# The first chunk of an attention-and-GLU kernel, taken through its first products in two halves

## The chip, the cores and the metric

One NeuronCore of one Trainium2 chip runs the whole kernel. The metric is device time in microseconds (us) of one execution; three executions of the kernel before took 2569.12, 2570.12 and 2572.28 us, median 2570.12. Engines are called as in the profile: PE is TensorE, with PEld its weight loads, DVE VectorE, ACT ScalarE, POOL GpSimd, SP SyncE, whose queue issues nearly all DMAs.

## The reference, cut to what matters

```python
# x: 1 x 2048 x 576, wqkv: 576 x 1728, wo: 576 x 576, H = 32 heads of 18
# w_gate, w_up: 576 x 4608, w_down: 4608 x 576
xn = layernorm(x)                       # over the 576 features, eps 1e-5
q, k, v = split(xn @ wqkv)              # per head
s = softmax(q @ k.T * 18 ** -0.5) @ v @ wo
g = silu(((xn @ w_gate) * (xn @ w_up)) @ w_down)
out = x + s * g
```

## The kernel before

All products run in a 32-bit matmul format, with each factor split into a high part (the copy that the engine's rounding leaves) and a low part (what is missing). A product of two split factors is three products, high by high, high by low and low by high; over the 576 features, in 4 slices of 128 and one of 64, `PAIRS` lists 14 of them.

The program has three stages. The prologue normalises x, turns it so that features lie on the partitions, and computes q, k and v of all rows. It goes by chunks of 512 rows (`NCH` = 4), each four tiles of 128 rows, and by nine blocks of 128 q and k columns. The main stage, from about 200 us on, runs scores, softmax, values and the GLU's products on PE in an order that a planner inside the kernel works out from assumed durations. The last stage multiplies by wo and adds. The change touches the first chunk of the prologue alone, where each engine takes its instructions in the order in which the program writes them.

Before, chunk 0 goes through these steps. `load_x(c)` fetches four tiles of x (L269), `w_fetch(i)` the raw weights of two blocks, `w_last(i, at, b)` one 64-row rest of a block's weights. `norm(0)` takes the tiles one after another: `norm_stats` (L278 to L280) has DVE's statistics and ACT's square root, `norm_apply` (L288 to L292) DVE's reciprocal and scale, ACT's normalised tile `xn` and POOL's copy of its last 64 columns. `w_now(0)` splits the weights of blocks 0 and 1: for these two DVE makes the high part (L428), POOL the low part (L431). `to_columns(0)` turns the tiles: 20 transposes of 128 x 128 (L325), tile by tile, into five PSUM banks; then for each of the five feature slices ACT copies the bank into the high part of `xcx` (L337, L341) and DVE subtracts for the low part (L338, L342). Then `w_now(1)` splits blocks 2 and 3 (ACT L430, POOL L431), `norm(1)` normalises chunk 1, and in the loop over chunks `qk_block(b, 0)` for b = 0, 1, 2 runs 14 products of 512 columns each (L348), ACT's copy of the bank (L351), DVE's subtraction (L352) into `hl`, and the write of `hl` to DRAM (`sqk`, L358). `to_columns(1)` turns chunk 1 (L334), and blocks 3 to 5 of chunk 0 follow. `v_split` and `v_block` (L393, L394, L402) are the value weights and products.

The low parts of one block's weights and the rest of block 1 are read by its last five products:

```python
PAIRS = ([(i, i) for i in range(4)] + [(i, 4 + i) for i in range(4)] + [(8, 8)]
         + [(4 + i, i) for i in range(4)] + [(9, 8)])
```

Of the kernel before, what the change touches and what calls it, by code (L numbers as in the profile page):

```python
# [20 lines left out]
FT = mybir.dt.float32  # L21
FR = mybir.dt.float32r
I32 = mybir.dt.int32
AF = mybir.ActivationFunctionType
OP = mybir.AluOpType
# [15 lines left out]
def kernel(  # L41
# [10 lines left out]
    nc = tc.nc  # L52
    _, S, D = x.shape
# [8 lines left out]
    scale = float(DH) ** -0.5  # L62
# [9 lines left out]
    xcp = ctx.enter_context(tc.tile_pool(name="xcp", bufs=2))  # L72
# [12 lines left out]
    def bank(tag, bufs, k=None):  # L85
        if tag == "g":
            if k is None:
                k = turns[0] = (turns[0] + 1) % 4
            return psum.tile([128, 512], FT, name="pg", tag=f"g{k}", bufs=1)
        return psum.tile([128, 512], FT, name="p" + tag, tag=tag, bufs=bufs)  # L90
# [4 lines left out]
    ident = consts.tile([128, 128], FT, name="ident")  # L95
# [158 lines left out]
    xcs = [None] * NCH  # L254
    vstack, pro, early = ExitStack(), ExitStack(), ExitStack()
    ep = early.enter_context(tc.tile_pool(name="early", bufs=1, side="right"))
# [4 lines left out]
    pp = pro.enter_context(tc.tile_pool(name="pro", bufs=1))  # L261
    blocks = [0, 512, 128, 640, 256, 768, 384, 896, 1024]
    wq = {}
    xin, xns = {}, {}

    def load_x(c):
        xin[c] = ep.tile([128, 4, D], FT, name="xin", bufs=2)
        for t in range(4):
            nc.sync.dma_start(xin[c][:, t, :], x2[c * 512 + t * 128:c * 512 + t * 128 + 128, :])  # L269

    stat = {}

    def norm_stats(c, t):
        st = ep.tile([128, 2, 6], FT, name="st", bufs=4)
        mv = ep.tile([128, 2], FT, name="mv", bufs=4)
        rs = ep.tile([128, 3], FT, name="rs", bufs=4)
        for g in range(2):
            nc.vector.bn_stats(st[:, g, :], xin[c][:, t, g * HALF:(g + 1) * HALF])  # L278
        nc.vector.bn_aggr(mv, st)
        nc.scalar.activation(rs[:, 0:1], mv[:, 1:2], AF.Sqrt, bias=eps)  # L280
        stat[c, t] = mv, rs
# [18 lines left out]
    def norm(c, ts=range(4)):  # L300
        lag = 1 if c in FIRST else len(ts)
        for t in ts:
            norm_stats(c, t)
            if t - lag in ts:
                norm_apply(c, t - lag)
        for t in ts[-lag:]:
            norm_apply(c, t)

    nqk = [0]

    def to_columns(c):

        xn = xns.pop(c)
        if c < 2:
            xc = pp.tile([128, 9, 512], FR, name="xcx", bufs=2)
        else:
            xc = xcp.tile([128, 9, 512], FR, name="xc")
        xcs[c] = xc
        ps = {}
        if c == 0:  # L320
            for k in range(5):
                ps[k] = bank("g", 3) if k < 4 else bank("a", 2)
            for t in range(4):
                for k in range(5):
                    nc.tensor.transpose(ps[k][:, t * 128:(t + 1) * 128], xn[:, t, k * 128:(k + 1) * 128], ident)  # L325
        for k in range(5):
            if c:
                if k in (3, 4):
                    ps[k] = bank("a" if nqk[0] % 2 else "b", 2)
                    nqk[0] += 1  # L330
                else:
                    ps[k] = bank("g", 3)
                for t in range(4):
                    nc.tensor.transpose(ps[k][:, t * 128:(t + 1) * 128], xn[:, t, k * 128:(k + 1) * 128], ident)  # L334
            p = ps[k]
            if k < 4:
                nc.scalar.activation(xc[:, k, :], p, AF.Copy)  # L337
                nc.vector.tensor_tensor(xc[:, 4 + k, :], p, xc[:, k, :].bitcast(FT),  # L338
                                        op=OP.subtract)
            else:  # L340
                nc.scalar.activation(xc[:, 8, :], p, AF.Copy)  # L341
                nc.vector.tensor_tensor(xc[64:128, 8, :], p[64:128, :],  # L342
                                        xc[64:128, 8, :].bitcast(FT), op=OP.subtract)
    def qk_block(b, c):
        p = bank("a" if nqk[0] % 2 else "b", 2)
        nqk[0] += 1
        for n, (a, e) in enumerate(PAIRS):
            nc.tensor.matmul(p, wq[b, a], xcs[c][:, e, :], start=n == 0,  # L348
                             stop=n == len(PAIRS) - 1)
        hl = pp.tile([128, 2, 512], FR, name="hl", bufs=3)  # L350
        nc.scalar.activation(hl[:, 0, :], p, AF.Copy)  # L351
        nc.vector.tensor_tensor(hl[:, 1, :], p, hl[:, 0, :].bitcast(FT), op=OP.subtract)  # L352
        g0 = blocks[b]
        for kind in range(2):
            lo, hi = max(g0, kind * D), min(g0 + 128, (kind + 1) * D)
            if lo < hi:
                dst = sqk[kind, :, lo - kind * D:hi - kind * D, c * 512:(c + 1) * 512]
                nc.sync.dma_start(dst.rearrange("h r s -> r h s"), hl[lo - g0:hi - g0].bitcast(FT))  # L358


    def x_part(b, part):
        return divmod(2 * b + part, 9)
# [61 lines left out]
    def w_piece(i, at, n, b, k0, src):  # L424

        w, low = w_tile(i)
        if i == 0 and b < 2:
            nc.vector.tensor_copy(w[:, at:at + n, :], src)  # L428
        else:
            nc.scalar.activation(w[:, at:at + n, :], src, AF.Copy)  # L430
        nc.gpsimd.tensor_tensor(w[:, low + at:low + at + n, :], src, w[:, at:at + n, :].bitcast(FT), op=OP.subtract)  # L431
        for k in range(k0, k0 + n):
            wq[b, k if k < 4 else 8] = w[:, at + k - k0, :]
            wq[b, 4 + k if k < 4 else 9] = w[:, low + at + k - k0, :]

    def w_now(i):
        at = 0
        for b, n in WHOLE[i]:
            w_piece(i, at, n, b, 0, raws[i][:, at:at + n, :])
            at += n  # L440
# [8 lines left out]
    def w_last(i, at, b):  # L449

        raw = ep.tile([128, 1, 128], FT, name="wl", bufs=2)
        w_load(raw, b, 4, 5)
        return lambda: w_piece(i, at, 1, b, 4, raw)

    def x_store(c, ks):
        for k in ks:
# [3 lines left out]
            else:  # L460
                for part in range(2):
                    nc.sync.dma_start(sx[c, 8, :, part, :], src[64 * part:64 * part + 64])

    def x_first(b, part):

        i, k = x_part(b, part)
        j, r0 = (4 * part + b // 2, 64 * (b % 2)) if b < 8 else (8, 64 * part)
        for r in (0, 64):
            nc.sync.dma_start(xg[i][r:r + 64, k, :].bitcast(FT), xcs[0][r0:r0 + 64, j, :].bitcast(FT))

    raws = {}
    load_x(0)
    w_fetch(0)
    last1 = w_last(2, 9, 1)
    load_x(1)
    w_fetch(1)
    last3 = w_last(2, 10, 3)
    norm(0)
    w_now(0)
    last1()  # L480
    to_columns(0)
    w_now(1)
    norm(1)
    last3()
# [3 lines left out]
    for c in range(NCH):  # L488
        if c + 2 < NCH:
            load_x(c + 2)  # L490
        for b in range(3):
            qk_block(b, c)
        if c + 1 < NCH:
            to_columns(c + 1)
        if c == 0:
            w_now(2)
            last5()
        for b in range(3, 6):
            qk_block(b, c)
            if b < 5 and c + 2 < NCH:  # L500
                norm(c + 2, (0, 1) if b == 3 else (2, 3))
            if c in (1, 2):
                x_store(c, range(3 * (b - 3), 3 * (b - 2)))
            if (c, b) in ((0, 3), (1, 3)):
                v_split(c)
            if (c, b) == (0, 5):
                v_fetch(1)
            if c == NCH - 1 and b == 3:
                w_now(3)
        if c == 1:  # L510
            w_fetch(3)
            for t in range(4):
                v_block(t)
            w_fetch(4)
            last7 = w_last(4, 5, 7)
        if c == 2:
            w_now(4)
            last7()
# [37 lines left out]
    n = 8  # L556
# [21 lines left out]
    with ExitStack() as mid:  # L578
# [240 lines left out]
        def high(k, c):  # L819
            if k == 0:  # L820
                hi[c] = fin["ep"].tile([128, 5, 512], FR, name="hi", bufs=2)
            nc.scalar.activation(hi[c][:, k, :], lo[k][:, 512 * c:512 * c + 512].bitcast(FT), AF.Copy)

        def low(k, c):
            part = lo[k][:, 512 * c:512 * c + 512]
            if k < 4:
                nc.vector.tensor_tensor(part, part.bitcast(FT), hi[c][:, k, :].bitcast(FT), op=OP.subtract)
            else:
                nc.vector.tensor_tensor(hi[c][64:128, 4, :], part[64:128].bitcast(FT), hi[c][64:128, 4, :].bitcast(FT),
                                        op=OP.subtract)  # L830
# [67 lines left out]
        turn = {"a": 0, "b": 0}  # L898
# [300 lines left out]
    ep = fin["ep"]  # L1199
# [63 lines left out]
    ps = {t: banks_of(t) for t in range(4)}  # L1263
# [6 lines left out]
    for t in range(NT):  # L1270
# [5 lines left out]
        for _ in range((2, 0, 0, 0, 2, 2, 1, 0, 2, 2, 1, 0, 0, 0, 0, 0)[t]):  # L1276
            if split:
                k, c = split.pop(0)
# [35 lines left out]
```

## Time and profile before

| | us |
|---|---|
| median of three executions | 2570.12 |
| the profiled execution | 2571.43 |
| its span in the trace | 2569.4 |
| PE busy in the span | 2547.8 (99%) |
| identity ready (DVE, L259) | 1.38 |
| first instruction of PE | 6.79 |
| last product of chunk 0's blocks 0 to 2, start of chunk 1's transposes | 23.23 |

Times below are us from the start of the span. A row of the timeline gives the start, the time it covers, the engine, the line, the operation with its output and inputs, and how many it merges; in brackets stands the idle time before it and what ended it. A line with "L" is a line of the kernel before. PE's matmuls are pipelined: the distance between the starts is what one costs in a stream, and the single duration is longer.

### The profile page before, as it was taken

The page shows a single profiled execution, that of the slowest core. Times are in us where ns is not written, and L with a number is a line of the kernel's source. Part 1 is how long each engine was busy: PE and PEld are TensorE (multiplying, and loading weights), DVE is VectorE, ACT ScalarE, POOL GpSimd, SP SyncE. Part 2 cuts the span into 40 slices and gives each one's busy share as a digit, 9 for nine tenths or more (in the row PEclk, how much of TensorE's full clock was granted, in tenths as well). Part 3 has the DMA queues.
Part 4 walks back from the last instruction along what each step waited for, and adds up shares of the span by engine and source line. Part 5 has one row for each costly group of instructions (what it writes and reads, how often), then busy time and mean ns, then how long its engine had stood idle before and what let it go on. Part 6 is the DMA issues. An engine that isn't in the chain of part 4 may idle for free.

```text
span 2569.4 us, 59203 instructions
## 1 busy us (share of the span) xinstructions
PE 2547.8 (99%) x24360; PEld 2111.1 (82%) x24360; DVE 1933.2 (75%) x3377; ACT 1467.1 (57%) x2688; POOL 594.8 (23%) x663
## 2 busy tenths in 40 slices
PE   8999999999999999999999999999999999999999
PEld 7899888878878888877888888777888877888878
DVE  6208778777778898777778888777888887778437
ACT  5222666666756665555665665555665655556651
POOL 3214434434421111111111111111111111111125
PEclk9999999999999999999999999999999999999999
DMA  7799988888886666665686656665686666654567
GB/s 243 235 284 278 263 226 225 232 225 220 221 206 186 176 182 177 175 179 155 179 197 173 179 175 184 176 170 154 179 204 166 180 184 176 175 174 146 159 189 248
DMA packets 195898, 504.58 MB, mean 196 GB/s; under 512 B 58112, under 2 KB 116352, under 8 KB 156588
## 3 DMA queue, kind: packets, MB, share of 16 engines
q1 hardware_dynamic: 185676, 489.05, 68.6%
q0 software_dynamic: 9952, 11.74, 1.7%
q8 instruction: 192, 3.15, 0.6%
q14 instruction: 78, 0.64, 0.1%
HBM read 312.21 MB, written 107.61 MB: 163 GB/s over the span
## 4 chain that ended last, share of the span: by engine, by line
PE 95%; DMA 3%; DVE 1%; SPq 0%; ACT 0%; issue 0%; POOL 0%; ACTq 0%; DVEq 0%
PE pg L678 34%; PE pg L639 18%; PE pg L720 16%; PE pa L596 12%; PE pb L628 8%; PE pg L402 2%; PE pa L348 2%; PE pb L348 2%; PE pg L1244 1%; DMA hx<-hs 1%; PE pb L1244 1%; PE pa L1244 1%; DMA sqk<-hl 0%; DMA ring<-sqk 0%; DMA xc<-sx 0%; DMA o<-sot 0%
## 5 line engine op out<-in xcount | busy, mean ns | idle before, releaser
L598 DVE TENSOR_REDUCE mx<-pa 128x1 f32<-128x512 f32 x2048 | 1367.1, 686 | 223.6 <-PE pa L596 104.8
L630 ACT ACTIVATE pt<-pb 128x512 f32<-128x512 f32 x2048 | 1161.9, 598 | 534.8 <-PE pb L628 465.5
L678 PE MATMUL pg<-xc,wgu 64*128 64x512 f32 x7776 | 1366.1, 388 | 0.7 <-DMA xc<-sx 0.5
L678 PEld LDWEIGHTS pg<-xc,wgu 64*128 64x128 f32 x7776 | 1051.7, 184 | 41.6 <-DMA xc<-sx 1.2
L628 PE MATMUL pb<-pair,ring 64*128 64x512 f32 x1997 | 777.4, 395 | 1.5 <-DMA ring<-sqk 1.5
L596 PE MATMUL pa<-pair,ring 64*128 64x512 f32 x2006 | 776.9, 393 | 1.8 <-DVE mx L598 1.8
L720 PE MATMUL pg<-wd,hs 64*128 64x288 f32 x3408 | 523.4, 292 | 0.0
L720 PE MATMUL pg<-wd,hx 64*128 64x288 f32 x3408 | 515.2, 292 | 2.4 <-DMA hx<-hs 2.4
L694 POOL TENSOR_TENSOR hs<-us,hs 128x512 fp32r<-128x512 f32 x144 | 186.2, 1293 | 1320.3 <-ACT hs L693 1285.6
L720 PEld LDWEIGHTS pg<-wd,hs 64*128 64x128 f32 x3408 | 459.8, 185 | 4.0 <-DVE acc L748 0.2
L720 PEld LDWEIGHTS pg<-wd,hx 64*128 64x128 f32 x3408 | 453.4, 185 | 6.5 <-DMA hx<-hs 3.0
L639 PE MATMUL pg<-pt,vt 128*32 128x512 f32 x4096 | 454.8, 594 | 0.7 <-DVE acc L748 0.6
L596 PEld LDWEIGHTS pa<-pair,ring 64*128 64x128 f32 x2006 | 364.3, 184 | 69.8 <-issue 52.8
L628 PEld LDWEIGHTS pb<-pair,ring 64*128 64x128 f32 x1997 | 362.5, 184 | 8.7 <-issue 1.9
L639 PEld LDWEIGHTS pg<-pt,vt 128*32 128x32 f32 x4096 | 125.5, 110 | 284.0 <-issue 278.9
L748 DVE TENSOR_TENSOR acc<-acc,pg 128x288 f32<-128x288 f32 x544 | 233.0, 443 | 22.4 <-PE pg L720 21.4
L645 DVE TENSOR_TENSOR oc<-oc,pg 128x512 f32<-128x512 f32 x69 | 47.1, 683 | 220.4 <-PE pg L639 213.7
L693 ACT ACTIVATE hs<-us 128x512 fp32r<-128x512 f32 x144 | 91.0, 632 | 151.0 <-DVE us L690 149.7
L194 POOL TENSOR_TENSOR wgu<-wraw,wgu 128x384 fp32r<-128x384 f32 x108 | 108.6, 1017 | 97.1 <-ACT wgu L193 84.6
L643 ACT ACTIVATE oc<-pg 128x512 f32<-128x512 f32 x32 | 19.2, 598 | 185.0 <-PE pg L639 179.0
L690 DVE TENSOR_TENSOR us<-pg,us 128x512 f32<-128x512 f32 x144 | 98.2, 682 | 26.9 <-PE pg L678 15.7
L618 POOL DMA_DIRECT2D pair<-mt x128 | 77.8, 613 | 166.4 <-DVE mt L613 162.3
(141 smaller groups left out, 1359.0 us busy)
## 6 DMA issues: line engine op xcount, KB each, us to landing
wgu<-swg SPq DMA_DIRECT2D x102, 1152.0 KB
hx<-hs SPq DMA_DIRECT2D x142, 512.0 KB
wd<-swd SPq DMA_DIRECT2D x50, 1152.0 KB
swg<-wgu SPq DMA_DIRECT2D x36, 1152.0 KB
pair<-sqk SPq DMA_DIRECT2D x192, 144.0 KB
ring<-sqk SPq DMA_DIRECT2D x384, 72.0 KB
swd<-wd SPq DMA_DIRECT2D x18, 1152.0 KB
sqk<-hl SPq DMA_DIRECT2D x32, 512.0 KB
```

The costliest lines, as they stand in the source:

```text
L194: nc.gpsimd.tensor_tensor(w[:, 9 + b:12 + b, :], raw[:, b:b + 3, :], w[:, b:b + 3, :].bitcast(FT), op=OP.subtract)
L348: nc.tensor.matmul(p, wq[b, a], xcs[c][:, e, :], start=n == 0, stop=n == len(PAIRS) - 1)
L596: nc.tensor.matmul(p, q[rows, t * 128:(t + 1) * 128], k[rows, c * 512:(c + 1) * 512], start=True, stop=True)
L598: nc.vector.tensor_reduce(mx[h][:, t, c:c + 1], p, axis=AX.X, op=OP.max)
L628: nc.tensor.matmul(p, k[rows, t * 128:(t + 1) * 128], q[rows, c * 512:(c + 1) * 512], start=True, stop=True)
L630: nc.scalar.activation(pt[t, c], p, AF.Exp, scale=scale)
L639: nc.tensor.matmul(p[32 * c:32 * c + 32, :], vt[h // 2][:, t, 6 * (h % 2):6 * (h % 2) + 32], pt[t, c], start=t == ts[0], stop=t == ts[-1])
L678: nc.tensor.matmul(ps, gw[n][half[r], a, :], xg[i][half[r], e, :], start=k == 0, stop=k == len(TERMS) - 1)
L690: nc.vector.tensor_tensor(h32, ps, h32, op=OP.mult)
L694: nc.gpsimd.tensor_tensor(hj[:, 1, :], h32, hj[:, 0, :].bitcast(FT), op=OP.subtract)
L720: nc.tensor.matmul(ps[:, 0:HALF], (hx if k else hs)[u][half[r], j, a, s * 128:(s + 1) * 128], dw[u][half[r], k, j, e, :], start=n == 0, st ...
L748: nc.vector.tensor_tensor(a, a, ps[:, 0:HALF], op=OP.add)
```

## The change

Chunk 0 goes through a function of its own, `first_products`. PE first runs 26 transposes of the identity into a bank that nobody reads. Tiles 0 and 1 are normalised (tile 0 on ACT, tile 1 on DVE), turned, copied and subtracted in 256 columns, and multiplied with blocks 0 and 1; tiles 2 and 3 follow in the same way, the normalisation of tile 2 on ACT and of tile 3 on DVE, between the parts of the first half. The output of blocks 0 and 1 (`qk_end`) then comes before the weights of blocks 2 and 3 and before the normalisation of chunk 1, and the loop over chunks begins with block 2. SP's loads come in the order tiles 0 and 1, blocks 0 and 1, tiles 2 and 3, blocks 2 and 3, chunk 1; the third pair of weight blocks, the value weights and x of chunk 2 now stand behind the writes of blocks 0 and 1.

```diff
-    def load_x(c):
-        xin[c] = ep.tile([128, 4, D], FT, name="xin", bufs=2)
-        for t in range(4):
+    def load_x(c, ts=range(4)):
+        if c not in xin:
+            xin[c] = ep.tile([128, 4, D], FT, name="xin", bufs=2)
+        for t in ts:
             nc.sync.dma_start(xin[c][:, t, :], x2[c * 512 + t * 128:c * 512 + t * 128 + 128, :])
...
     def qk_block(b, c):
         p = bank("a" if nqk[0] % 2 else "b", 2)
         nqk[0] += 1
+        qk_product(b, c, p, slice(0, 512))
+        qk_end(b, c, p)
+
+    def qk_product(b, c, p, cols):
         for n, (a, e) in enumerate(PAIRS):
-            nc.tensor.matmul(p, wq[b, a], xcs[c][:, e, :], start=n == 0,
+            nc.tensor.matmul(p[:, cols], wq[b, a], xcs[c][:, e, cols], start=n == 0,
                              stop=n == len(PAIRS) - 1)
+
+    def qk_end(b, c, p):
         hl = pp.tile([128, 2, 512], FR, name="hl", bufs=3)
...
+    def first_products():
+
+        xn = xns[0] = ep.tile([128, 4, 640], FT, name="xn", bufs=1)
+        xc = xcs[0] = c_tile(0)
+        ps = [bank("g", 3) if k < 4 else bank("a", 2) for k in range(5)]
+        out = [bank("b", 2), bank("a", 2)]
+        nqk[0] += 2
+        idle = bank("b", 2)
+        for n in range(26):
+            nc.tensor.transpose(idle[:, 0:128], ident, ident)
+
+        def scales(t):
+            mv, rs = stat[0, t]
+            nc.vector.reciprocal(rs[:, 1:2], rs[:, 0:1])
+            if t % 2 == 0:
+                nc.vector.scalar_tensor_tensor(rs[:, 2:3], mv[:, 0:1], -1.0, rs[:, 1:2], op0=OP.mult, op1=OP.mult)
+
+        def apply(t):
+            mv, rs = stat.pop((0, t))
+            if t % 2 == 0:
+                nc.scalar.activation(xn[:, t, 0:D], xin[0][:, t, :], AF.Identity, scale=rs[:, 1:2], bias=rs[:, 2:3])
+            else:
+                nc.vector.tensor_scalar(xn[:, t, 0:D], xin[0][:, t, :], mv[:, 0:1], rs[:, 1:2],
+                                        op0=OP.subtract, op1=OP.mult)
+            nc.gpsimd.tensor_copy(xn[:, t, D:640], xn[:, t, 512:D])
+
+        def turn(g):
+            for ks in (range(4), (4,)):
+                for t in (2 * g, 2 * g + 1):
+                    for k in ks:
+                        nc.tensor.transpose(ps[k][:, t * 128:(t + 1) * 128], xn[:, t, k * 128:(k + 1) * 128], ident)
+
+        def high(g, k):
+            cols = slice(256 * g, 256 * g + 256)
+            nc.scalar.activation(xc[:, k if k < 4 else 8, cols], ps[k][:, cols], AF.Copy)
+
+        def low(g, k):
+            cols = slice(256 * g, 256 * g + 256)
+            rows, d, e = (slice(0, 128), k, 4 + k) if k < 4 else (slice(64, 128), 8, 8)
+            nc.vector.tensor_tensor(xc[rows, e, cols], ps[k][rows, cols], xc[rows, d, cols].bitcast(FT), op=OP.subtract)
+
+        for t in (0, 1):
+            norm_stats(0, t)
+        for t in (0, 1):
+            scales(t)
+            apply(t)
+        w_piece(0, 0, 5, 0, 0, raws[0][:, 0:5, :])
+        turn(0)
+        for k in range(5):
+            high(0, k)
+        for k in range(3):
+            low(0, k)
+        norm_stats(0, 2)
+        for k in range(3, 5):
+            low(0, k)
+        scales(2)
+        apply(2)
+        w_piece(0, 5, 4, 1, 0, raws[0][:, 5:9, :])
+        last1()
+        norm_stats(0, 3)
+        scales(3)
+        apply(3)
+        for b in range(2):
+            qk_product(b, 0, out[b], slice(0, 256))
+        turn(1)
+        for k in range(5):
+            high(1, k)
+            low(1, k)
+        for b in range(2):
+            qk_product(b, 0, out[b], slice(256, 512))
+            qk_end(b, 0, out[b])
+        xns.pop(0)
...
-    load_x(0)
+    load_x(0, (0, 1))
     w_fetch(0)
     last1 = w_last(2, 9, 1)
-    load_x(1)
+    load_x(0, (2, 3))
     w_fetch(1)
     last3 = w_last(2, 10, 3)
-    norm(0)
-    w_now(0)
-    last1()
-    to_columns(0)
+    load_x(1)
+    first_products()
     w_now(1)
     norm(1)
     last3()
...
-        for b in range(3):
+        for b in range(0 if c else 2, 3):
             qk_block(b, c)
```

`to_columns` loses its branch for chunk 0; the other chunks are unchanged in it.

On PE, chunk 0 begins so in the kernel before, from its last tile's transposes to chunk 1's (pg, pa and pb are PSUM banks, wgu and wq weight blocks):

```order
L325 MATMUL pg<-ident,xn 128x128 x4
L325 MATMUL pa<-ident,xn 128x128
L348 MATMUL pb<-xcx,wgu 128x512 x14
L348 MATMUL pa<-xcx,wgu 128x512 x8
L348 MATMUL pa<-xcx,wq_174 128x512
L348 MATMUL pa<-xcx,wgu 128x512 x4
```

and in the changed kernel from its first instruction on:

```order
L472 MATMUL pb<-ident 128x128 x26
L493 MATMUL pg<-ident,xn 128x128 x8
L493 MATMUL pa<-ident,xn 128x128 x2
L345 MATMUL pb<-xcx,wgu 128x256 x14
L345 MATMUL pa<-xcx,wgu 128x256 x8
L345 MATMUL pa<-xcx,wq_217 128x256
L345 MATMUL pa<-xcx,wgu 128x256 x4
```

The transposes of tiles 2 and 3, which stood ahead of the first product, now stand behind the first halves of blocks 0 and 1, and the same ten and 28 instructions follow once more.

On DVE, where chunk 0's low parts end and chunk 1's statistics begin, the kernel before has:

```order
L428 CAST wgu<-wraw 128x640
L428 CAST wgu<-wraw 128x512
L338 TENSOR_TENSOR xcx<-pg,xcx 128x512 x4
L342 TENSOR_TENSOR xcx<-pa,xcx 64x512
L278 BN_STATS st<-xin 128x6 x2
L279 BN_AGGR mv<-st 128x2
```

and the changed kernel:

```order
L427 CAST wgu<-wraw 128x512
L279 BN_STATS st<-xin 128x6 x2
L280 BN_AGGR mv<-st 128x2
L476 RECIPROCAL rs<-rs 128x1
L485 TENSOR_SCALAR xn<-xin,mv,rs 128x576
L502 TENSOR_TENSOR xcx<-pg,xcx 128x256 x4
L502 TENSOR_TENSOR xcx<-pa,xcx 64x256
L351 TENSOR_TENSOR hl<-pb,hl 128x512
L351 TENSOR_TENSOR hl<-pa,hl 128x512
L279 BN_STATS st<-xin 128x6 x2
```

The first statistics here are tile 3's of chunk 0, the last row is chunk 1's: it moved behind the second half's low parts and behind the outputs of blocks 0 and 1.

On ACT, at the same place, the kernel before has:

```order
L430 ACTIVATE wq_174<-wl 128x128
L337 ACTIVATE xcx<-pg 128x512 x4
L341 ACTIVATE xcx<-pa 128x512
L430 ACTIVATE wgu<-wraw 128x640
L430 ACTIVATE wgu<-wraw 128x512
L280 ACTIVATE rs<-mv,eps 128x1 x2
```

and the changed kernel:

```order
L497 ACTIVATE xcx<-pg 128x256 x4
L497 ACTIVATE xcx<-pa 128x256
L350 ACTIVATE hl<-pb 128x512
L350 ACTIVATE hl<-pa 128x512
L429 ACTIVATE wgu<-wraw 128x640
L429 ACTIVATE wgu<-wraw 128x512
L281 ACTIVATE rs<-mv,eps 128x1 x2
```

The weights of blocks 2 and 3, and with them the square roots of chunk 1, moved behind the copies of both output banks.

## Rows read from the trace of the kernel before

**Rows 1.** The page, the engines' busy time (part 1).

```profile
PE 2547.8 (99%) x24360; PEld 2111.1 (82%) x24360; DVE 1933.2 (75%) x3377; ACT 1467.1 (57%) x2688; POOL 594.8 (23%) x663
```

**Rows 2.** PE's waits, whole program: total us, times, longest.

```profile
PE pg L325 <- ACT xn L291: 7.4, 2, 6.8
PE pg L720 <- DMA hx<-hs: 2.4, 2, 2.2
...
PE pg L402 <- POOL wv L394: 0.4, 1, 0.4
```

**Rows 3.** The chain of waits, 12 to 26 us: start, us, what.

```profile
12.11 2.48 DVE xcx L338 x4
...
15.37 1.66 PE pb L348 x6
17.02 3.19 PE pa L348 x14
...
23.39 1.31 PE pg L334 x12
```

**Rows 4.** Timeline of PE: the fourth tile's transposes, chunk 1's.

```profile
11.02 1.06 PE L325 MATMUL pg<-ident,xn 128*128 128x128 f32 x4
11.87 0.41 PE L325 MATMUL pa<-ident,xn 128*128 128x128 f32 x1
23.23 1.47 PE L334 MATMUL pg<-ident,xn 128*128 128x128 f32 x12
```

**Rows 5.** Timeline of ACT, 5 to 34 us.

```profile
5.87 0.87 ACT L291 ACTIVATE xn<-xin,rs 128x576 f32<-128x576 f32 x1
15.05 1.26 ACT L430 ACTIVATE wgu<-wraw 128x640 fp32r<-128x640 f32 x2 [1.01 <-DMA wraw<-in_A_wqkv_dram]
21.22 1.63 ACT L291 ACTIVATE xn<-xin,rs 128x576 f32<-128x576 f32 x2
22.95 0.58 ACT L351 ACTIVATE hl<-pb 128x512 fp32r<-128x512 f32 x1
32.28 1.77 ACT L393 ACTIVATE wv<-wvraw 128x288 fp32r<-128x288 f32 x5
```

**Rows 6.** Timeline of DVE; the last row is the page's group of 288-column additions.

```profile
15.35 0.82 DVE L278 BATCH_NORM_STATS2 st<-xin 128x6 f32<-128x288 f32 x2
17.40 1.31 DVE L290 SCALAR_TENSOR_TENSOR rs<-mv,rs 128x1 f32<-128x1 f32 x1
23.56 0.69 DVE L352 TENSOR_TENSOR hl<-pb,hl 128x512 fp32r<-128x512 f32 x1 [1.90 <-ACT hl L351]
30.06 0.81 DVE L278 BATCH_NORM_STATS2 st<-xin 128x6 f32<-128x288 f32 x2
L748 DVE TENSOR_TENSOR acc<-acc,pg 128x288 f32<-128x288 f32 x544 | 233.0, 443 | 22.4 <-PE pg L720 21.4
```

**Rows 7.** Timeline of POOL: a 128-column weight subtraction, the pair of blocks 2 and 3.

```profile
13.61 0.47 POOL L431 TENSOR_TENSOR wq<-wl,wq 128x128 fp32r<-128x128 f32 x1
15.86 2.83 POOL L431 TENSOR_TENSOR wgu<-wraw,wgu 128x640 fp32r<-128x640 f32 x2 [1.78 <-ACT wgu L430]
```

**Rows 8.** The chain of waits from 130 us: products of 288 columns.

```profile
131.50 29.71 PE pg L402 x224
```

**Rows 9.** Timeline of PE at a late pause; then stretches (PEclk is the granted clock).

```profile
2512.16 0.40 PE L1244 MATMUL pa<-wos,o 128*128 128x288 f32 x1 [0.20 <-DVE o L827]
2513.77 1.06 PE L1244 MATMUL pa<-wos,hi 128*128 128x288 f32 x4 [1.20 <-DVE hi L829]
2514.00:2517.50 3.50, 3.50 (x16) 3.50 (x16) 2.61 (x5) 2.12 (x5) 0.00 (x0) 0.52 1.05 322
276.00:278.00 2.00, 1.76 (x21) 1.74 (x21) 0.92 (x2) 0.79 (x2) 0.00 (x0) 1.00 0.96 219
```

**Rows 10.** SP's queue, then a stretch: the last two numbers are DMA share and GB/s.

```profile
13.68 0.37 SPq L104 DMA_DIRECT2D wraw<-in_A_wqkv_dram  x1
34.00:36.00 2.00, 2.00 (x10) 1.65 (x10) 1.97 (x4) 0.52 (x2) 2.00 (x3) 1.00 0.00 0
```

More of the change, by code (lines that the diff above doesn't have):

```diff
@@ L309, with c_tile @@
     nqk = [0]
+    def c_tile(c):
+        if c < 2:
+            return pp.tile([128, 9, 512], FR, name="xcx", bufs=2)
+        return xcp.tile([128, 9, 512], FR, name="xc")
     def to_columns(c):
         xn = xns.pop(c)
[L314 to L322, printed above, removed]
-            for t in range(4):
[L324 to L335, printed above, removed]
+        xc = xcs[c] = c_tile(c)
+        for k in range(5):
+            if k in (3, 4):
+                p = bank("a" if nqk[0] % 2 else "b", 2)
+                nqk[0] += 1
+            else:
+                p = bank("g", 3)
+            for t in range(4):
+                nc.tensor.transpose(p[:, t * 128:(t + 1) * 128], xn[:, t, k * 128:(k + 1) * 128], ident)
             if k < 4:
@@ L462, in x_store @@
                     nc.sync.dma_start(sx[c, 8, :, part, :], src[64 * part:64 * part + 64])
+    def first_products():
[16 more added lines that the diff above has]
+                nc.scalar.activation(xn[:, t, 0:D], xin[0][:, t, :], AF.Identity, scale=rs[:, 1:2], bias=rs[:, 2:3])
+            else:
+                nc.vector.tensor_scalar(xn[:, t, 0:D], xin[0][:, t, :], mv[:, 0:1], rs[:, 1:2],
[37 more added lines that the diff above has]
+        turn(1)
+        for k in range(5):
+            high(1, k)
[4 more added lines that the diff above has]
+        xns.pop(0)
```

## The prediction, made before the changed kernel ran

> **What bounds the kernel now.** I read the page's first part first: TensorE (PE) is busy 99% of the span [rows 1]. Of its waits over the whole program one stands out, 6.8 us at the start for the first normalised tile, the next is 2.2 us [rows 2]. So what PE loses early comes back nowhere, unless a later wait is shortened; the only one that it puts between 24 and 200 us is 0.4 us, for POOL's share of a value weight (L402). The chain around the change shows who feeds PE: from 12.11 to 15.3 VectorE's (DVE's) low parts of chunk 0, from 15.37 on PE alone, block 0's last six products, blocks 1 and 2, then chunk 1's transposes at 23.39 without a pause [rows 3]. They do not pause because chunk 1 is just ready: DVE starts its statistics at 15.35 [rows 6] and ScalarE (ACT) ends its last two tiles at 21.22 + 1.63 = 22.85 [rows 5]. That is 0.4 us before PE asks: the reader should see that **the normalisation of chunk 1 has no slack**. The change lets PE begin earlier, but also moves that normalisation.
>
> **The idle transposes.** The identity is there at 1.4 (table above). Before, the transposes of the fourth tile take (11.87 − 11.02)/4 = 0.2125 us each, chunk 1's take 1.31/12 = 0.109 [rows 3, 4]: the first are at 1.2 GHz, the second at 2.4 (the page's clock row reads full speed for both; the pitch decides). 26 at 0.2125 are 5.5 us and end at 6.9. What covers them is the wait for tile 0, which ACT ends at 5.87 + 0.87 = 6.74 [rows 5] (tile 1, on DVE, about the same): they cost 0.1–0.2 us. In the trace full speed came with the first product at 12.1, after transposes from 6.8 on; here PE has been at work since 1.4 when the first real transpose comes, so I take 0.109 for it and keep 0.2125 as the other end.
>
> **First half.** Bank 0 is whole after five transposes and some 0.2 us of drain: 7.65. A 256-column copy on ACT I estimate at 0.30 us apiece from the 288-column ones, (1.77 − 0.43)/4 = 0.33 [rows 5]; a 256-column subtraction on DVE at 0.33 apiece and 0.41 alone, from 0.60 and 0.69 at 512 columns and 0.44 at 288 [rows 3, 6]. DVE has the first three low parts done at 9.05; then tile 2's statistics stand in its queue (0.82 + 0.21, 0.97 before the next may start), so the last two low parts end at 10.75, tile 2's scales at 11.05, the second weight cast at 11.4, tile 3's statistics at 12.4, its scale and subtraction at 13.4. PE's products of block 0 need all five low parts: six are left at 10.75. A 256-column product I take at 0.12 us (288 columns: 29.71/224 = 0.133, 512: 3.19/14 = 0.228 [rows 3, 8]). Block 1's first half reaches its low weights at 12.6 and waits for GpSimd (POOL): tile 2 applied on ACT by 11.9, its copy (a quarter of a microsecond for 64 columns, my estimate from the 128-column row), the 512-column weight subtraction, 512/1152 of the pair's 2.83, 1.3, the 128-column one 0.47 [rows 7], that is 14.0. DVE's subtraction for tile 3 falls into that stretch; a DVE instruction next to a POOL subtraction was held 1.31 us and ended with it [rows 6, 7], so 0.3 us go to one or the other. Block 1's first half ends at **14.4**.
>
> **Second half.** Only then may PE turn tiles 2 and 3, since its queue is in order. Bank 0 is whole at 15.15, DVE's five low parts run from 15.55 to 17.3, and 6 + 14 products of 0.12 follow: block 1 ends at **19.8**. Before it ended at 20.2 [rows 3]. The split itself is nearly free on PE (56 × 0.12 against 28 × 0.228, +0.3 us), and the head start of six microseconds is spent on waiting for DVE and POOL twice in place of once.
>
> **The moved normalisation.** On DVE the statistics of chunk 1 now stand behind both output subtractions of blocks 0 and 1. ACT's copy of block 1's bank takes 0.6, DVE's subtraction 0.69 [rows 5, 6]: they start at 21.05, **5.7 us later** than 15.35. The second pair of weight blocks now also stands behind these copies on ACT: it starts at 20.3 and not 15.05, its POOL subtractions (2.83 us) run from 21.05 to 23.9. Tile 0's scale comes in that stretch as before, when it ended at 18.71 with POOL at 18.69 [rows 6, 7]: 23.9, 5.2 later. From there the work is unchanged, 22.85 − 18.71 = 4.14 us: chunk 1 is ready at 28.05. PE needed its fourth tile at 23.23 + 3 × 0.109 = 23.56 [rows 4]; block 2 ends at 21.05 + 3.2 = 24.3. So PE stands nearly idle from 24.3 to 28.1 with three lone transposes, and everything behind shifts by 28.1 − 23.56 = **+4.5 us**. Ends: +3.8 if POOL does not hold the scale (then it ends at 21.05 + 2.05 + 0.16 = 23.26, 0.65 less), +6.3 if the first transposes are at half clock (+0.6) and the thin stretch from 8 to 11 lets the clock fall, with 15 products at 0.24 and the end of block 1's first half at 15.6 (+1.2). I take 4.5, from the rows of the same instructions.
>
> **The clock in that pause.** At 2512.16 PE issued one product between idle times of 0.2 and 1.2 us; from 2514 to 2517.5 the granted clock was 0.52, and 16 products took 3.5 us where 16 × 0.133 = 2.1 would do: 1.4 us lost. But a pause of 2.2 us before 276.2 left it at 1.00 [rows 2, 9]. The new pause is 3.8 us, longer than either, so I take 1.4; ends 0 and 2.65, half of the slow stretch from 6.8 to 12.1. The Trainium skill, "TensorE: Matmul & The Clock Gate", section "HAM oscillation — how this bites in real kernels", says that a wait between groups of matmuls throttles PE again and the next group starts slow; by it the sum keeps the 1.4 us, by the pause before 276.2 it would be 4.5 alone. That page speaks against this change; the trace agrees with it at 2514 and not at 276.2.
>
> **Loads.** x of chunk 1 now comes behind the second pair of weight blocks; it is wanted at 21, and before it was there by 15.35 at the latest [rows 6], with one pair of weight blocks less ahead of it. SyncE's queue (SP) has the writes of blocks 0 and 1 (3 DMAs) ahead of the third pair of weight blocks: issue at about 22 in place of 13.68 [rows 10], and the value weights and x of chunk 2, in the same order behind them, eight microseconds later too. Cost nothing: their user on DVE starts at 30.06 [rows 6] and moves to about 36, and the stretch from 34 to 36, DMA share 0.00, shows room for the moved traffic [rows 10]. Were that cover gone, DVE's chain of chunk 2 would be late by the excess. DVE and ACT have two output blocks fewer in front of chunk 1's banks, which can only take back the 0.4 us wait [rows 2]. **Sum:** 4.5 + 1.4 = 5.9 us. The profiled execution took 2571.43 (span 2569.4 and 2.0 around it) and would take 2577.3; it was 1.3 above the median 2570.12, from which I forecast **2576.0 us**. 0.2%, 5.1 us, is about what a measurement of this kernel can tell from no change.
>
> **Rivals.** *The clock stays up* in the pause, as at 276.2: +4.5 (3.8 to 5.2), 2574.6, mostly within 0.2%. For it: three transposes fall into the pause. Against: 2512, where one product did not help. *The thin stretch too is slow*: products of the first halves at 0.24 and a second fall, 6.3 + 1.4 to 2.65, 2577.8 to 2579.1. For it: by the working above PE has a dozen products of 0.12 between 8 and 11. *Not slower*: PE turns tiles 2 and 3 early, because tile 3 and POOL's weights are ready near 12.1 and not 14.4; the 2.3 us come off block 1's end, POOL is through before the scale (0.65), the pause shrinks to under 2 us and the clock stays: +1.6, 2571.7. It decides at 12.1; against it are two statistics and a cast in DVE's queue ahead of tile 3. *Faster by over 0.2%* PE's own work excludes: 20 × 0.109 + 56 × 0.12 + 14 × 0.228 = 12.1 us from 6.9 end at 19.0, 4.2 before 23.2; only a later wait could add to it.
>
> **How the numbers follow.** Forecast with pause and fall 0.60 (+4.9 to +8), clock stays 0.20, slow thin stretch 0.12, not slower 0.06, faster 0.02. Over 5.1 us lie nearly nine tenths of the forecast, a fifth of the second case and all of the third, 0.70; within 0.2% the rest, 0.28. The range runs from 2572.8 (a clock that stays and a free scale, less a microsecond between runs) to 2579.8; it leaves out the last two cases and little more. The forecast's own range is 2575 to 2578.1.
>
> **What would show it.** The new profile should have ten transposes near 6.9 at 0.109 apiece, second-half transposes at 14 to 15, DVE's first statistics of chunk 1 at about 21, PE waiting for ACT's tiles until about 28, a granted clock of 0.5 for some microseconds at 28 to 31, and the same shift at every later stage. Wrong it is if chunk 1's transposes come before 25, or if the shift at 60 us is not the shift at the end.

## The result, and the profile after

Sixteen executions of the changed kernel took 2574.0 to 2579.98 us, median **2577.3**; sixteen of the kernel before, taken beside them, 2569.12 to 2574.45, median 2571.9. The ratio is 1.002 (95%: 1.0013 to 1.0027), +5.4 us, by the interval +3.3 to +6.9: **slower, by just over 0.2%**, and inside the range. The profiled execution took 2575.41 us, its span is 2573.3.

The page of the changed kernel, the engines' busy time, beside [rows 1]:

```profile
PE 2553.4 (99%) x24414; PEld 2110.5 (82%) x24414; DVE 1934.1 (75%) x3382; ACT 1465.3 (57%) x2691; POOL 593.8 (23%) x663
```

PE has 54 instructions more, the 26 idle transposes and 28 products cut in two. What counts is what it waits for. Its waits, as in [rows 2] (total us, times, longest):

```profile
PE pg L328 <- ACT xn L292: 2.5, 4, 0.9
...
PE pb L472 <- DVE ident L259: 1.4, 1, 1.4
PE pb L345 <- ACT wgu L429: 1.3, 1, 1.3
PE pb L345 <- DVE xcx L502: 0.8, 1, 0.8
PE pa L345 <- POOL wgu L430: 0.8, 1, 0.8
PE pg L493 <- ACT xn L483: 0.6, 1, 0.6
...
PE pg L790 <- DMA hx<-hs: 0.5, 1, 0.5
```

The first wait is 1.4 us, for the identity, in place of 6.8 for tile 0, and five smaller ones have come behind it: for ACT's chunk 1 (2.5), ACT's copies of block 2's weights (1.3), DVE's low parts (0.8), POOL's weights (0.8) and tile 0 (0.6), 6.0 together. Where they lie shows the timeline of PE:

```profile
1.44 4.85 PE L472 MATMUL pb<-ident 128*128 128x128 f32 x26 [1.44 <-DVE ident L259]
6.88 1.09 PE L493 MATMUL pg<-ident,xn 128*128 128x128 f32 x8 [0.59 <-ACT xn L483]
...
10.50 1.44 PE L345 MATMUL pb<-xcx,wgu 128*128 128x256 f32 x7 [0.81 <-DVE xcx L502]
...
13.78 0.74 PE L345 MATMUL pa<-xcx,wgu 128*128 128x256 f32 x4 [0.76 <-POOL wgu L430]
...
14.64 1.04 PE L493 MATMUL pg<-ident,xn 128*128 128x128 f32 x8
...
21.69 3.47 PE L345 MATMUL pb<-xcx,wgu 128*128 128x512 f32 x14 [1.31 <-ACT wgu L429]
25.65 0.33 PE L328 MATMUL pg<-ident,xn 128*128 128x128 f32 x1 [0.49 <-ACT xn L292]
26.71 0.33 PE L328 MATMUL pg<-ident,xn 128*128 128x128 f32 x1 [0.73 <-ACT xn L292]
27.93 0.33 PE L328 MATMUL pg<-ident,xn 128*128 128x128 f32 x1 [0.89 <-ACT xn L292]
28.69 1.87 PE L328 MATMUL pg<-ident,xn 128*128 128x128 f32 x9 [0.43 <-ACT xn L292]
```

Chunk 1's transposes are the three lone ones and the nine behind them. The fourth, at 23.23 + 3 × 0.109 = 23.56 before [rows 4], is now at 28.69: **+5.13 us**. Who holds them shows the timelines of the three engines that feed PE, to be set beside [rows 5 to 7]:

```profile
20.42 0.60 ACT L350 ACTIVATE hl<-pa 128x512 fp32r<-128x512 f32 x1 [1.07 <-PE pa L345]
20.91 1.25 ACT L429 ACTIVATE wgu<-wraw 128x640 fp32r<-128x640 f32 x2
...
27.02 1.61 ACT L292 ACTIVATE xn<-xin,rs 128x576 f32<-128x576 f32 x2
```

```profile
9.11 0.81 DVE L279 BATCH_NORM_STATS2 st<-xin 128x6 f32<-128x288 f32 x2
...
13.16 0.88 DVE L485 TENSOR_SCALAR xn<-xin,mv,rs 128x576 f32<-128x576 f32 x1
...
21.05 0.69 DVE L351 TENSOR_TENSOR hl<-pa,hl 128x512 fp32r<-128x512 f32 x1 [0.98 <-ACT hl L350]
21.66 0.81 DVE L279 BATCH_NORM_STATS2 st<-xin 128x6 f32<-128x288 f32 x2
...
23.70 0.86 DVE L291 SCALAR_TENSOR_TENSOR rs<-mv,rs 128x1 f32<-128x1 f32 x1
```

```profile
12.45 1.27 POOL L430 TENSOR_TENSOR wgu<-wraw,wgu 128x512 fp32r<-128x512 f32 x1
...
21.72 2.82 POOL L430 TENSOR_TENSOR wgu<-wraw,wgu 128x640 fp32r<-128x640 f32 x2 [7.18 <-ACT wgu L429]
```

The chain reads backwards from ACT's last two tiles (28.63) to tile 0's scale, which DVE ends at 24.56 with POOL at 24.54, to chunk 1's statistics at 21.66, to the subtraction of block 1's output, to ACT's copy at 20.42, to PE's last product. Before, the statistics stood at 15.35 [rows 6], with no output ahead of them.

The clock behind the pause, in stretches (PEclk is the third number from the end):

```profile
28.00:30.00 2.00, 1.57 (x9) 1.38 (x10) 0.66 (x2) 2.00 (x5) 0.84 (x3) 0.76 0.81 175
30.00:32.00 2.00, 2.00 (x12) 2.00 (x10) 1.92 (x4) 1.49 (x3) 0.00 (x0) 0.50 1.02 315
32.00:34.00 2.00, 2.00 (x10) 1.65 (x9) 1.39 (x2) 1.74 (x5) 0.40 (x1) 0.88 0.99 319
```

From about 29 to 32 PE had the lower level, 1.2 GHz. Block 3 starts at 32.27 instead of 25.58: +6.69, of which 5.13 is the pause and 1.56 the clock. The shift then stays. The chain of waits of the changed kernel, its value products and two rows at the end:

```profile
138.15 29.71 PE pg L401 x224
...
2518.11 1.20 PE pa L1314 x7
2519.30 1.32 PE pb L1314 x10
```

The 224 value products started at 131.50 [rows 8]: +6.65. The span grew by only 3.9, and three later places say why. PE waited 0.5 us for `hx`, up to 281.26, not the 2.2 of before, up to 276.24 [rows 2, 9]: the next long row of the chain moves from 299.36 to 304.25, +4.89. At the late pause of [rows 9] the products of 2513.77 come at 2518.11, +4.34, and the clock stays up, so that the 17 products above take 2.5 us where they had taken 4.05: +2.8. From the last result on DVE to the span's end it is 4.5 us in place of 3.4: +3.9. The change touches none of these places; the medians of sixteen executions each put the difference at +5.4.

### The profile page after: what moved, and what is told of

Read it like the earlier page. It is cut to its first block, busy times and chain, and to the rows that moved or that the text cites. A ratio compares the mean times of both kernels' runs of the same rounds, so it can differ in the third digit from the quotient of the medians.

```text
span 2573.3 us, 59321 instructions
## 1 busy us (share of the span) xinstructions
PE 2553.4 (99%) x24414; PEld 2110.5 (82%) x24414; DVE 1934.1 (75%) x3382; ACT 1465.3 (57%) x2691; POOL 593.8 (23%) x663
## 4 chain that ended last, share of the span: by engine, by line
PE 94%; DMA 2%; DVE 2%; SPq 0%; issue 0%; ACT 0%; POOL 0%; ACTq 0%; DVEq 0%; POOLq 0%
PE pg L748 34%; PE pg L709 18%; PE pg L790 16%; PE pa L666 11%; PE pb L698 8%; PE pg L401 2%; PE pa L345 2%; PE pb L345 2%; PE pg L1314 1%; PE pb L1314 0%; PE pa L1314 0%; DMA sqk<-hl 0%; DMA hx<-hs 0%; DVE mx L668 0%; DMA ring<-sqk 0%
```

## The experiments

**Theory.** The loss is the moved normalisation of chunk 1: 4.5 us of pause, 1.4 of clock. **Rivals.** The split of chunk 0 loses in itself (its waits of 0.8 us, the 256-column products); the loads' order costs; the clock alone decides.

Each time is the median beside that of the kernel before, measured with it. "Shift" is that of the 224 value products against 131.50 [rows 8], in one profile each. It has the prologue's effect in it, but also what PE waited for value weights a little earlier (0.3 us in the changed kernel's profile, 1.0 in its third), and the clock differs between executions: three profiles of the changed kernel gave +6.65, +5.46 and +7.69, a second one of the kernel before −0.16. A difference of 2 us between two shifts shows nothing by itself; the starts within the prologue, given below, are steadier.

| kernel | us (before) | ratio, 95% | shift |
|---|---|---|---|
| the change | 2577.3 (2571.9) | 1.0013 to 1.0027 | +6.65 |
| moved_norm_alone | 2576.97 (2571.11) | 1.0014 to 1.0032 | +5.29 |
| bridge | 2574.36 (2571.11) | 1.0004 to 1.0021 | +5.16 |
| no_idle | 2578.38 (2571.11) | 1.0017 to 1.0038 | +8.01 |
| early_norm | 2579.47 (2571.11) | 1.002 to 1.0043 | +9.26 |
| early_norm_early_loads | 2572.7 (2570.46) | 1.0 to 1.0018 | +1.77 |
| changed_early_loads | 2576.64 (2570.46) | 1.0017 to 1.0038 | +5.58 |
| idle_alone | 2570.89 (2570.46) | 0.9992 to 1.0009 | −0.76 |
| loads_alone | 2574.61 (2570.46) | 1.0003 to 1.002 | +2.75 |

**The move alone.** The kernel before, chunk 0 unsplit, without idle transposes and with the old order of the first loads; only blocks 0 and 1 come ahead of the weights of blocks 2 and 3 and of the normalisation. Their writes thereby also stand ahead of the third pair's loads on SP, which are issued at 22.49 in place of 13.68, as they are at 23.18 in the changed kernel:

```diff
     to_columns(0)
+    for b in range(2):
+        qk_block(b, 0)
     w_now(1)
     norm(1)
...
-        for b in range(3):
+        for b in range(0 if c else 2, 3):
```

> The kernel before, unsplit and without idle transposes, in which blocks 0 and 1 with their outputs are merely put ahead of the weights of blocks 2 and 3 and of chunk 1's normalisation, as the changed kernel has it. Theory: this alone makes the whole loss: chunk 1's statistics near 21.6, ready near 28.6, a pause of about 4 us with a clock of 0.5 behind it, block 3 near 32.3, time +5 to +6 us on the kernel before, the same as the changed kernel. Rival (the split costs and the move is partly free): block 3 starts before 29.5, time +3 or less.

The same pause, from the timeline of PE and the stretches of this kernel:

```profile
27.32 0.33 PE L334 MATMUL pg<-ident,xn 128*128 128x128 f32 x1 [0.88 <-ACT xn L291]
28.08 2.18 PE L334 MATMUL pg<-ident,xn 128*128 128x128 f32 x9 [0.43 <-ACT xn L291]
```

```profile
28.00:30.00 2.00, 1.92 (x9) 1.92 (x10) 1.27 (x2) 1.74 (x5) 0.68 (x2) 0.50 0.86 231
```

The fourth transpose is 4.52 us later, of the change's 5.13, block 3 starts at 31.71 (+6.13, of 6.69), and the time is +5.9 us, what the prediction's sum had come to. This move alone makes nearly the whole loss; the split, the idle transposes and the first loads together add 0.6 us at the fourth transpose, nothing that the times can tell. The weights of blocks 2 and 3 move with the normalisation; no run moves one without the other.

**The clock's share.** In the changed kernel 30 idle transposes go between block 2 and chunk 1's, to fill the pause:

```diff
             qk_block(b, c)
+        if c == 0:
+            spare = bank("g", 1, turns[0])
+            for n in range(30):
+                nc.tensor.transpose(spare[:, 0:128], ident, ident)
         if c + 1 < NCH:
             to_columns(c + 1)
```

> The changed kernel, with 30 more idle transposes between block 2 and the transposes of chunk 1, so that the pause is filled with work that nobody reads. Theory (the clock falls in the pause and costs 1.5 us of the 6.7): granted clock 1.00 from 28 to 33, chunk 1's fourth transpose still at 28.7, block 3 starts near 30.7 in place of 32.27, 1.5 us less in all. Rival (the slow transposes are bound by something else, such as ScalarE's copies or VectorE): the clock is 1.00 and block 3 still starts near 32.

The timeline of PE there, with the pause filled and the twelve transposes at (29.91 − 28.46)/12 = 0.12 us apiece:

```profile
25.19 3.44 PE L566 MATMUL pg<-ident 128*128 128x128 f32 x30
28.46 1.61 PE L328 MATMUL pg<-ident,xn 128*128 128x128 f32 x12
```

The granted clock was 1.00 from 26 to 32, block 3 starts at 30.95, 1.3 before the changed kernel's. The pause's length is still lost: block 3 is 5.4 later than before, and the time is still +3.25 us (by the interval +1.0 to +5.4). The clock is the small part, the late tiles the large one.

**The normalisation put back.** The weights of blocks 2 and 3 and chunk 1's normalisation come ahead of the outputs of blocks 0 and 1 (the idle transposes write block 0's bank, so that a bank is free):

```diff
             qk_product(b, 0, out[b], slice(256, 512))
+        w_now(1)
+        norm(1)
+        last3()
+        for b in range(2):
             qk_end(b, 0, out[b])
...
     first_products()
-    w_now(1)
-    norm(1)
-    last3()
     w_fetch(2)
```

> The changed kernel, but the weights of blocks 2 and 3 and the normalisation of chunk 1 come again ahead of the outputs of blocks 0 and 1 (the idle transposes go to block 0's own bank). Theory (the moved normalisation costs the time): VectorE starts chunk 1's statistics near 17.6 in place of 21.66, chunk 1 is ready near 24.6, TensorE's pause shrinks from 3.8 to about 1 us, the clock stays at 1.00, block 3 starts near 26.6 (before 25.58, changed 32.27), and the time is 1 us over the kernel before, some 5 under the changed one. Rival (the split itself costs, since VectorE and GpSimd are waited for twice): block 3 still starts 4 us or more behind the kernel before and the time stays at about +4.

The pause went as expected: statistics at 18.07, fourth transpose at 24.89, block 3 at 26.90 (25.33 before, in the same timeline). But the kernel is no faster than the changed one (+8.4 us against +5.4), for a wait that I had not seen coming, in the timelines of PE, ACT and SP:

```profile
34.77 5.06 PE L345 MATMUL pb<-xcx,wq 128*128 128x512 f32 x14 [4.40 <-ACT wq L429]
```

```profile
33.98 1.36 ACT L429 ACTIVATE wq<-wraw 128x640 fp32r<-128x640 f32 x2 [5.06 <-DMA wraw<-in_A_wqkv_dram]
```

```profile
26.27 1.92 SPq L357 DMA_DIRECT2D sqk<-hl  x3
28.28 0.85 SPq L104 DMA_DIRECT2D wraw<-in_A_wqkv_dram  x1
```

The third pair of weight blocks stands on SP behind the writes `sqk` of the outputs, which now wait until 26; meanwhile the DMA engines rest:

```profile
20.00:22.00 2.00, 2.00 (x14) 1.74 (x13) 1.90 (x9) 1.36 (x4) 0.88 (x2) 1.00 0.01 4
22.00:24.00 2.00, 2.00 (x11) 1.57 (x9) 1.43 (x7) 1.84 (x5) 0.34 (x2) 1.00 0.00 0
24.00:26.00 2.00, 1.57 (x13) 1.25 (x12) 0.45 (x1) 2.00 (x6) 0.91 (x3) 1.00 0.00 0
```

So the order of the loads is free in the changed kernel only because the pause covers it. Two kernels hold this apart: the third pair, the value weights and x of chunk 2 are issued ahead of the writes, once with the normalisation put back, once in the changed kernel as it is.

```diff
         apply(3)
+        third_loads()
...
+    def third_loads():
+        w_fetch(2)
+        last.append(w_last(2, 11, 5))
+        v_fetch(0)
+        load_x(2)
...
-    w_fetch(2)
-    last5 = w_last(2, 11, 5)
-    v_fetch(0)
...
```

> The early normalisation of the run early_norm, and the loads of the third pair of weight blocks, of the value weights and of chunk 2's x issued again ahead of the writes of blocks 0 and 1. Theory (with the pause gone, the loads queued behind those writes were the new last wait: 4.4 us at block 4 and a fall of the clock): no wait of TensorE at block 4, block 3 near 26.9, first value product near 61.9 (before 60.58 for the first long run), time 1 to 2 us over the kernel before. Rival (something in the split or in the early order keeps TensorE waiting later): time still 4 us or more over the kernel before.

> The changed kernel with these same loads ahead of the writes of blocks 0 and 1, and nothing else. Theory (in the changed kernel the late loads are hidden by the pause, so they cost nothing there): block 3 at 32.3 as in the changed kernel, time the same as the changed kernel's, within 1 us, +5 to +6.5. Rival (the late loads slow a later stage by their traffic): 2 us or more under the changed kernel.

With both, PE no longer waits at block 4, and the timeline shows the rest of the loss:

```profile
20.55 3.37 PE L345 MATMUL pb<-xcx,wgu 128*128 128x512 f32 x14
23.76 0.67 PE L328 MATMUL pg<-ident,xn 128*128 128x128 f32 x3
24.86 1.20 PE L328 MATMUL pg<-ident,xn 128*128 128x128 f32 x9 [0.43 <-ACT xn L292]
```

Block 2 starts at 20.55, 0.5 after its start before (20.06 in the same timeline): even without pause and load wait the split gains nothing, and chunk 1 is still 1.3 us late. The clean comparison is with changed_early_loads, which differs from it only in the place of the normalisation with the weights ahead of it, and in the bank of the idle transposes, and whose clock stayed up too: 24.86 against 28.75 at the fourth transpose, 3.9 us, and +1.77 against +5.58 in the shift; the times are +2.2 (0 to +4.6) against +6.2 (+4.4 to +9.8). (The profiled execution of early_norm_early_loads, 2566.61 us, was the shortest of eleven, the others 2570.64 to 2574.5; PE waits 0.7 us for `hx` in it and, where the kernel before waits 1.5 us for `ring`, not at all.) In the changed kernel the early loads change nothing that shows: fourth transpose at 28.75, time +6.2. Block 3 came at 30.83 and not at 32.3, since the clock did not fall.

**The idle transposes**, taken out of the changed kernel, and added alone to the kernel before:

```diff
-        for n in range(26):
+        for n in range(0):
             nc.tensor.transpose(idle[:, 0:128], ident, ident)
```

```diff
     raws = {}
+    idle = bank("b", 2)
+    for n in range(26):
+        nc.tensor.transpose(idle[:, 0:128], ident, ident)
     load_x(0)
```

> The changed kernel without the 26 idle transposes. Theory (they buy the warm clock for the first ten transposes and little else, since VectorE's queue bounds the halves): the first ten transposes take 0.21 us each, bank 0 is ready 0.6 us later, blocks 0 and 1 end 0.6 to 2 us later than 20.4, block 3 starts near 33 to 34; time 0.5 to 2 us over the changed kernel. Rival (the idle transposes cost): time under the changed kernel's.

> The kernel before with the 26 idle transposes ahead and nothing else. Theory (they help the transposes, but chunk 1's normalisation has only 0.4 us of slack and the fourth tile of chunk 0 is bound by its own normalisation until 10.6): transposes at 0.109 us, bank 0 copied 0.4 us sooner, block 3 at 25.0 to 25.3 in place of 25.58, time 0 to 0.6 us under the kernel before, not to be told from it. Rival (the warm start carries through): 1.5 us or more gained.

Without them the first real transposes and products run slower, as PE's timeline shows, and block 1 ends at 21.8 and not 20.4:

```profile
6.88 1.97 PE L493 MATMUL pg<-ident,xn 128*128 128x128 f32 x8 [6.88 <-ACT xn L483]
...
12.96 1.91 PE L345 MATMUL pa<-xcx,wgu 128*128 128x256 f32 x8
```

Eight products of 256 columns in 1.71 us (the next starts at 14.67), 0.21 apiece; with the idle transposes 8 take 0.96 (11.78 to 12.74), 0.12 apiece. They are worth 1.4 us at block 1's end inside the change, and 0.8 at block 3 alone (24.78, where I had expected 25.0 to 25.3). Neither shows in the times: without them +7.3 us (+4.4 to +9.8) against the change's +5.4, alone +0.4 (−2.1 to +2.3).

**The loads' order alone**, in the kernel before:

```diff
-    load_x(0)
+    load_x(0, (0, 1))
     w_fetch(0)
     last1 = w_last(2, 9, 1)
-    load_x(1)
+    load_x(0, (2, 3))
     w_fetch(1)
     last3 = w_last(2, 10, 3)
+    load_x(1)
     norm(0)
```

> The kernel before with the changed kernel's order of the first loads (tiles 2 and 3 of chunk 0 behind blocks 0 and 1, chunk 1 behind blocks 2 and 3) and nothing else. Theory: the statistics of tile 2 start near 8.3 in place of 6.45 and chunk 0 is turned 1 to 1.5 us later, so that block 3 starts near 26.8 and the time is 1 to 1.5 us over the kernel before; in the changed kernel this is hidden by the first half. Rival (the loads land in time in either order): block 3 at 25.6.

The timeline of DVE has a wait at tile 2, and PE's next transposes come 3.04 us later for it:

```profile
9.03 0.82 DVE L279 BATCH_NORM_STATS2 st<-xin 128x6 f32<-128x288 f32 x2 [3.14 <-DMA xin<-in_A_x_dram]
```

I had expected 8.3, and with it block 3 near 26.8 and a loss of 1 to 1.5 us; block 3 starts at 28.15 and the time is +4.15 us (+0.8 to +5.1). Tile 2 is issued at 5.18 and used 3.85 us later, behind two blocks of weights. In the changed kernel the same statistics run at 9.11 without a wait, since DVE has just ended three low parts: there the order costs nothing, by a margin of 0.1 us if the tile lands as it does here.

**Two more executions of the changed kernel, one of the kernel before**, with no edit:

> The changed kernel once more, for a second trace of it. Theory (which part of the pause the clock sees, and the wait for hx near 276, differ between executions of one kernel): chunk 1's fourth transpose at 28.7 again within 0.3 us; block 3 at 32.3 if the clock falls and at 30.8 if it does not; the wait for hx either 0.5 or 2.2 us. Rival (both belong to the kernel): block 3 at 32.3 and the wait at 0.5 again.

> The changed kernel a third time, with the same expectations as for its second trace: chunk 1's fourth transpose at 28.7, block 3 at 32.3 or 30.8 by the clock, the wait for hx at 0.5 or 2.2 us.

> The kernel before once more, for a second trace of it. Theory: block 3 at 25.6 again within 0.3 us, since nothing in that stretch waits long enough for the clock to fall; the wait for hx near 276 either 0.5 or 2.2 us. Rival (the wait belongs to the kernel): 2.4 us again.

The changed kernel took 2574.89 and 2578.06 us. Both have the same pause and the same three lone transposes, the fourth at 28.72 and 28.62, but in the first the clock stayed up. The stretch from 30 to 32 of the one and of the other:

```profile
30.00:32.00 2.00, 2.00 (x14) 1.77 (x13) 2.00 (x5) 2.00 (x5) 0.00 (x0) 1.00 0.98 298
```

```profile
30.00:32.00 2.00, 2.00 (x12) 2.00 (x10) 1.86 (x3) 1.49 (x3) 0.00 (x0) 0.50 1.08 324
```

Block 3 starts at 30.80 and at 32.31: 1.5 us. Whether the clock falls in this pause belongs to the execution: of the three profiles of the changed kernel it fell in two, and it stayed up in the one of changed_early_loads (block 3 at 30.83). Why is open; no run here settles it. One thing goes with it: where the clock fell, the 26 idle transposes at the start had taken 4.85 and 4.77 us, where it stayed up 5.50 and 5.45, so these executions differ before 7 us already. That the one leads to the other is not shown. The kernel before, once more, had block 3 at 25.40. The waits for `hx` were 1.8 and 2.1 us in the changed kernel, 2.4 in the kernel before, as in its first profile.

## Why the prediction was right

It said 2576.0 against 2570.12, +5.9; measured is +5.4 between the medians, with the mechanism it named. By its own steps:

- *Idle transposes.* Expected to end at 6.9 and to cost 0.1 to 0.2. The first real transposes came at 6.88. In the profiled execution the clock rose while they ran, they ended at 6.3, and PE then waited 0.59 for ACT; in changed_again they took the 5.5 us that I had reckoned with.
- *First half.* Expected to end at 14.4 with PE waiting for DVE (last low part at 10.75) and POOL (12.6 to 14.0): it waited 0.81 before 10.50 and 0.76 before 13.78, and the second transposes came at 14.64. POOL's subtraction held tile 3 on DVE, as said.
- *Second half.* 19.8 expected, 20.4 measured. Of these 0.6 us, 0.24 were there at the second transposes; DVE's low parts run from 15.81 to 17.69, where I had 15.55 to 17.3 (0.39 at their end), and the last 20 products take 0.2 more. This is the term that was too small, and it runs through every later step.
- *Moved normalisation.* Statistics 21.66 (21.05 expected), tile 0's scale held by POOL until 24.56 (23.9), chunk 1 ready at 28.63 (28.05), the pause +5.13 (+4.5). Each is late by the same 0.6: the chain was right link by link. That this move alone is nearly the whole loss, moved_norm_alone shows, with 4.52 for the pause.
- *The clock in the pause.* 1.4 expected; where it falls, the way from the fourth transpose to block 3 took 1.56 to 1.67 longer than before. I took the fall because the pause is longer than the two of [rows 9], and the runs show that a wait's length does not decide it (last section): that the profiled execution had it was partly luck. I gave the case that it stays a chance of 0.20 for all executions alike; the runs show that it is no such choice, the same kernel does both. The Trainium skill, "TensorE: Matmul & The Clock Gate", section "HAM oscillation — how this bites in real kernels", says that a wait between groups of matmuls throttles PE again: two profiles of the changed kernel agree (0.50 at 30 to 32), the third does not (1.00).
- *Loads cost nothing.* True here, as changed_early_loads shows, and for the reason given, a cover: the third weight pair is wanted late because everything is late. early_norm shows the price without it, 4.4 us of wait at block 4, on PE through ACT's weights; I had named DVE's chain of chunk 2 as the place.
- *The rivals.* The slow thin stretch did not come: the first eight products of block 1's first half took 0.12 us each in the profiles of the changed kernel. It is no fixed property of the kernel either: in early_norm, whose instructions are the same up to there but for the bank of the idle transposes, the clock was 0.50 from 12 to 14, these eight took 0.21 each, and the second transposes came at 15.01 in place of 14.64. "Not slower" failed at its point: POOL's weights ended at 13.72, not near 12.1.
- *The test that I set.* "The shift at 60 us is not the shift at the end" holds for the profiled pair (+6.64 in the first long run of value products, at 67.22, +3.9 at the end), and yet the mechanism stands: the test was too strict, since a later wait for DMA differs by up to 1.6 us between executions of one kernel (`hx` in the changed kernel: 0.5, 1.8, 2.1). The clock at the late pause fell in both profiles of the kernel before and in none of the three of the changed one; whether that belongs to the kernels is open.

That the median rose by 5.4 and not by the profiled shift of 6.65 fits a clock that falls in part of the executions (+5.46 in the execution where it stayed, though +7.69 in the third, 1.0 of it behind block 3), and a late clock that stays up; the interval of 3.6 us is too wide to show either. No kernel that ran here beats the kernel before.

## What to carry to other kernels

Before a stage is started earlier, look at what its output steps are put in front of: in queues that run in order, a copy that ends a product must wait for that product, and everything written behind it waits too, here a normalisation with 0.4 us of slack. When a stall is removed, read each DMA queue for loads behind a write that waits for compute; a stall can be the only reason why they come in time. To tell such small changes apart, read a start within the stage: chunk 1's fourth transpose came at 28.62 to 28.72 in three profiles of one kernel, while the 224 value products behind the prologue differed by 2.2 us in them, and the total time by 6 us over sixteen executions.

## What the runs showed of the hardware that was not expected

- The same instructions with the same pause kept the granted clock at 1.00 in one execution and fell to 0.50 in two; the difference is 1.5 us at block 3. Elsewhere too the length of the wait does not decide. At the late pause the clock fell after 1.20 us in the kernel before [rows 9], but stayed at 1.00 after 1.17 in moved_norm_alone and after 1.74 in early_norm. At the wait for `hx` it stayed up after 2.23 us in the kernel before [rows 9] and fell after 2.45 in before_again, the same program, and after 2.05 in changed_third (0.72 from 284 to 286, 0.50 in the next two). PE's timeline and a stretch, first of moved_norm_alone, then of before_again:

```profile
2517.00 0.80 PE L1246 MATMUL pa<-wos,hi 128*128 128x288 f32 x4 [1.17 <-DVE hi L831]
2518.00:2520.00 2.00, 2.00 (x17) 2.00 (x16) 1.57 (x3) 0.86 (x2) 0.00 (x0) 1.00 1.04 285
```

```profile
276.48 0.60 PE L720 MATMUL pg<-wd,hx 64*128 64x288 f32 x1 [2.45 <-DMA hx<-hs]
276.00:278.00 2.00, 1.52 (x11) 1.52 (x13) 0.19 (x1) 0.60 (x1) 0.00 (x0) 0.59 0.90 355
```

- With loads waiting on SP behind a write, the DMA share was 0.00 to 0.01 from 20 to 26 us in early_norm, before a wait of 4.4 us for one of these loads. In early_norm_early_loads, where they are issued from 14.07 on, it was 0.70 to 1.05 from 14 to 24.
- A scale of 128 x 1 on DVE, 0.16 us at tile 1, took 0.86 next to POOL's subtraction and ended within 0.02 us of it; it did so in moved_norm_alone too (0.86).
